# Table loads, weight narrowing and first folds moved in the opening steps of an FNet and gated-convolution kernel

## Chip, cores, metric

The kernel runs on one core of a Trainium2 chip. The metric is the device time of one execution in microseconds (us), given as the median of several executions. A profiled execution is read from its trace, whose times count from the start of the span. In the profile PE is TensorE (PEld its weight loads), DVE is VectorE, ACT is ScalarE and POOL is GpSimd. PSUM is where the program's matrix products are put.

## The reference

The reference takes the real part of a two-dimensional Fourier transform of `x` (8 batches, 3136 positions, 256 features), multiplies by `w_in` (256 x 1024), applies relu, a three-tap convolution over positions with a sigmoid, the gate, and `w_out` (1024 x 256):

```python
X = np.fft.fft(np.fft.fft(x, axis=1), axis=2).real
h = np.maximum(X @ w_in, 0.0)                  # 8 x 3136 x 1024
conv = sum(conv_w[k] * shifted(h, k - 1) for k in range(3))
out = (h / (1.0 + np.exp(-conv))) @ w_out      # 8 x 3136 x 256
```

The inputs of the weights are float64 in memory and are narrowed to float32 on the chip.

## The kernel before

A batch goes through folding on VectorE (sums and differences of mirrored positions), nine transform units on TensorE with tables of cosines and sines (four for odd, four for even frequencies, one for a single feature), and then 32 steps of the feed-forward part: 4 chunks of positions times 8 blocks of features. The 8 x 32 = 256 steps are one pipeline. In cycle t each engine does a piece of steps t - 3 to t + 2, and work of the next batch, and at first of the weights, is put in at given cycles:

```python
for t in range(n + LAG):                       # LAG is 3
    ...
    products(steps[t + 1]); copies(steps[t + 1])   # PE, then ACT
    combine(steps[t])                              # DVE: relu(h), frees a PSUM buffer
    ...
    run("dve")                                     # narrowing and folds
    ...
    other_taps(steps[t - 1]); gate(steps[t - 2])   # DVE, and GpSimd for half of gate
    mm2(steps[t - 3])                              # PE: times w_out
    run("pe")                                      # blocks(i), transform of the next batch
```

A weight is narrowed by seven integer and float instructions of VectorE. `w_in` is narrowed in four quarters. `blocks(i)` then multiplies quarter i with the small feature transform `dm`, so that the feed-forward part can start from the sequence transform. `w_out` is narrowed in four quarters too, and `mm2` of the first eight steps needs one of them every second step. The parts that the change touches, cut:

```python
for par in (1, 0):                 # odd tables, then even tables
    load_tables(par)
    if par:
        w_in[0].load(nc.sync)
        nc.sync.dma_start(out=dm, in_=dft_dim[:, :, 0:2])
for i in (1, 2, 3):
    w_in[i].load(nc.sync)
...
keep_on(18)                        # dummy matmuls, meant to keep PE's clock up
mirror_tables(0); mend_row(1, half); mirror_tables(2)     # ACT, odd tables: fill in, scale one row
for i in range(4):
    for j, u in enumerate(odds):
        u.part(i)
        if i == 3:
            u.copy(); u.fin()      # ACT; DVE, frees the unit's PSUM buffer
            if j == 1:
                ...
                w_in[0].narrow(0, 2)
mend_row(0, half)                  # ACT, even tables
for i, u in enumerate(us[j] for j in (2, 4, 3, 7, 8)):
    u.matmuls(0, 1); u.copy(); u.fin()
    if i == 2:
        ...
        blocks(0)
keep_on(2)
w_in[1].narrow(0, 2)
...
for i in (1, 2, 3):
    if i > 1:
        at(2 * i - 2, "dve", lambda i=i: w_in[i].narrow(0, 2))
    at(2 * i - 2, "pe", lambda i=i: blocks(i))
for c in range(0, NF, 2):
    at(1 + c, "dve", lambda c=c: w_out.narrow(c, c + 2))
...
end = 5                            # first cycle with a fold of the next batch
```

In what follows "step 6" or "combine(6)" counts such cycles, and "first product" is the first matmul of step 0.

## Time and profile before

| | before |
|---|---|
| median of 3 runs | 1252.91 us (1252.37 to 1253.13) |
| PE, DVE, ACT, GpSimd busy, share of the span | 97%, 91%, 71%, 32% |
| first product of step 0 | 44.20 us |
| combine(19), right behind the last fold of batch 1 (step 18) | 157.19 us |

The page has the span in 40 slices of 31 us. Each digit is the busy share of a slice in tenths, and for PEclk the granted clock of PE:

```profile
PE   5999999999999999999999999999999999999998
...
DVE  6799989999999999998999988999999888899996
...
PEclk9989999999999999999999999999999999999999
```

PE and DVE are both over 90% nearly everywhere, so neither alone can be called the bound from this view. The third digit of PEclk, from 62 to 94 us, is the one place where the clock was not at its full speed for long (0.50 from 62.5 to 69.3 us). That is in the stretch that the change touches. Which engine sets the time in which part of it is read from the timelines, which the prediction shows.

### The profile page before, as it was taken

The numbers are of one execution on the slowest core, as the hardware profiler recorded it, in microseconds if no ns is written. First come the engines' busy times: TensorE is split into PE (matmuls) and PEld (weight loads), VectorE is DVE, ScalarE is ACT, GpSimd is POOL, SyncE is SP. The second block draws the span as 40 slices with busy tenths as digits, with TensorE's granted clock in tenths as the row PEclk, the third lists the DMA queues.
The fourth block names the chain that finished last, engine by engine and source line by source line (L and its number), as shares of the span: only waits on it lengthen the run. The fifth ranks groups of instructions, "written<-read, shape, count | busy, mean of one in ns | idle before, by whom it ended". The sixth has DMA issues, their size and how long they took to land.

```text
span 1250.0 us, 15703 instructions
## 1 busy us (share of the span) xinstructions
PE 1206.5 (97%) x4982; PEld 906.1 (72%) x4982; DVE 1140.6 (91%) x1691; ACT 885.1 (71%) x1843; POOL 398.1 (32%) x502
## 2 busy tenths in 40 slices
PE   5999999999999999999999999999999999999998
PEld 4557776677777767777677777777777777777776
DVE  6799989999999999998999988999999888899996
ACT  2436666776777776777777777777777778788885
POOL 5214432442524151332424215242322213122222
PEclk9989999999999999999999999999999999999999
DMA  9503121220302021110202012020010001100000
GB/s 237 162 1 96 34 78 57 73 70 9 97 33 82 26 69 29 59 52 26 91 32 62 28 52 71 26 85 26 1 45 33 30 26 40 32 28 31 26 26 29
DMA packets 47618, 65.86 MB, mean 53 GB/s; under 512 B 5740, under 2 KB 35204, under 8 KB 47536
## 3 DMA queue, kind: packets, MB, share of 16 engines
q1 hardware_dynamic: 42355, 51.98, 13.5%
q0 software_dynamic: 5120, 12.85, 3.6%
q8 instruction: 39, 0.64, 0.2%
q14 instruction: 43, 0.35, 0.1%
q10 hardware_dynamic: 61, 0.04, 0.0%
HBM read 39.06 MB, written 25.74 MB: 52 GB/s over the span
## 4 chain that ended last, share of the span: by engine, by line
PE 65%; DVE 20%; issue 5%; ACT 5%; POOL 1%; DMA 1%; SPq 0%; DVEq 0%; ACTq 0%; POOLq 0%
PE po L91 40%; PE pb L91 10%; PE pa L91 9%; DVE g L604 7%; PE pd L91 6%; DVE g L625 3%; DVE h L592 3%; ACT nb L581 2%; DVE xh L166 1%; ACT g L617 1%; DVE xh L155 1%; DVE w L182 1%; DVE w L183 1%; DVE xh L170 1%; DVE xh L171 1%
## 5 line engine op out<-in xcount | busy, mean ns | idle before, releaser
L91 PE MATMUL po<-wout,g 128*128 128x256 f32 x3072 | 711.0, 381 | 20.2 <-DVE g L625 16.3
L91 PEld LDWEIGHTS po<-wout,g 128*128 128x128 f32 x3072 | 577.4, 190 | 178.3 <-DVE g L625 53.1
L604 DVE SCALAR_TENSOR_TENSOR g<-h,cw,g 128x770 f32<-128x770 f32 (+1 forms) x512 | 555.3, 1084 | 10.7 <-ACT g L598 1.5
L624 POOL TENSOR_TENSOR g<-g,h 128x385 f32<-128x385 f32 (+1 forms) x256 | 240.5, 940 | 747.6 <-ACT g L617 525.9
L617 ACT ACTIVATE g<-g 128x385 f32<-128x385 f32 (+2 forms) x512 | 244.3, 527 | 200.6 <-DVE g L604 200.4
L581 ACT ACTIVATE nb<-pb 128x386 f32<-128x386 f32 (+2 forms) x472 | 208.1, 494 | 82.6 <-PE pb L91 81.2
L592 DVE CUSTOM_DVE_ANT_0 h<-pa,nb 128x386 f32<-128x386 f32 (+2 forms) x492 | 255.4, 559 | 5.3 <-ACT h L578 5.3
L598 ACT ACTIVATE g<-h,cw 128x770 f32<-128x770 f32 (+1 forms) x256 | 243.4, 951 | 0.2 <-DVE h L592 0.2
L91 PE MATMUL pb<-qt,G 127*128 127x387 f32 (+2 forms) x512 | 214.1, 499 | 0.4 <-ACT nb L581 0.2
L91 PE MATMUL pa<-pt,G 128*128 128x387 f32 (+2 forms) x512 | 211.8, 494 | 0.0
L625 DVE TENSOR_TENSOR g<-g,h 128x385 f32<-128x385 f32 (+1 forms) x256 | 151.8, 593 | 1.3 <-ACT g L617 1.3
L91 PEld LDWEIGHTS pa<-pt,G 128*128 128x128 f32 x512 | 96.9, 189 | 73.5 <-issue 18.9
L547 ACT ACTIVATE pa<-eb,ge 128x387 f32<-128x387 f32 (+2 forms) x248 | 149.2, 602 | 0.6 <-PE pa L91 0.6
L91 PE MATMUL pd<-tab,w 98*128 98x196 f32 (+3 forms) x448 | 117.4, 374 | 0.0
L91 PEld LDWEIGHTS pb<-qt,G 127*128 127x128 f32 x512 | 93.9, 190 | 22.6 <-issue 4.0
L130 POOL DMA_INDIRECT xh<-in_x_dram,idx x64 | 97.8, 1528 | 15.4 <-issue 12.2
L91 PEld LDWEIGHTS pd<-tab,w 98*128 98x128 f32 (+1 forms) x448 | 82.9, 190 | 12.8
L644 ACT COPY os<-po 128x256 f32<-128x256 f32 x196 | 58.0, 396 | 10.6 <-PE po L91 5.8
L155 DVE TENSOR_TENSOR xh<-xh 98x1020 f32<-98x1020 f32 (+1 forms) x32 | 45.7, 1433 | 2.4 <-DMA xh<-in_x_dram,idx 2.4
L166 DVE TENSOR_TENSOR xh<-xh 98x1024 f32<-98x1024 f32 (+1 forms) x32 | 41.4, 1294 | 0.1
L285 DVE TENSOR_TENSOR qt<-as,pd 128x197 f32<-128x197 f32 (+1 forms) x14 | 7.3, 519 | 24.9 <-ACT as L281 24.9
L347 POOL TENSOR_TENSOR er<-as 1x197 f32<-1x197 f32 (+1 forms) x16 | 12.5, 778 | 52.5 <-ACT as L339 46.0
(100 smaller groups left out, 456.6 us busy)
## 6 DMA issues: line engine op xcount, KB each, us to landing
out_dram<-os SPq DMA_DIRECT2D x192, 128.0 KB
xh<-in_x_dram SPq DMA_DIRECT2D x16, 784.0 KB
eb<-ed SPq DMA_DIRECT2D x16, 193.5 KB
tab<-dft_seq_dram SPq DMA_DIRECT2D x4, 589.5 KB
raw<-in_moe_w_in_dram SPq DMA_DIRECT2D x4, 512.0 KB
raw<-in_moe_w_out_dram SPq DMA_DIRECT2D x1, 2048.0 KB
eb<-ed SPq DMA_DIRECT2D x8, 209.0 KB
eb<-ed SPq DMA_DIRECT2D x7, 193.0 KB
```

The source lines that it names most:

```text
L91: nc.tensor.matmul(o, l, r, start=start, stop=stop, skip_group_check=True)
L130: nc.gpsimd.indirect_dma_start(out=xh[b, h][0:NP, 7 - m].rearrange("p q d -> p (q d)"), out_offset=None, in_=bass.AP(tensor=x.tensor, offs ...
L155: vt(a[:, :, :, 1:D], a[:, :, :, 1:D], r[:, :, :, D - 1:0:-1], op=ALU.add)
L547: act(pa[s][:, 0:n], eb[b, c], AF.Copy, scale=ge[:, f:f + 1])
L581: act(nb[s][:, i, cols], p[:, cols], AF.Copy, scale=-1.0 if i else 1.0)
L592: nc.vector._custom_dve(TENSOR_ADD_SAT, out=to, in0=a[:, cols], in1=c[:, i, cols], s0=BIG, s1=0.0)
L598: act(gs[s], hs[s][:, 0:n], AF.Copy, scale=cw[:, 0, s[2]:s[2] + 1])
L604: stt(out=g, in0=h[:, k:k + n], scalar=cw[:, k, f:f + 1], in1=g, op0=ALU.mult, op1=ALU.add)
L617: act(gs[s][:, c], gs[s][:, c], AF.Sigmoid)
L624: gt(g[:, p], g[:, p], h[:, p], op=ALU.mult)
L625: vt(g[:, v], g[:, v], h[:, v], op=ALU.mult)
L644: nc.scalar.copy(out=osb[:, j % 2], in_=pt[:, j % 2])
```

## The change

The intent is to remove idle time of PE and DVE in the first 160 us. The even tables are loaded directly behind the odd ones, so that `mend_row(0)` can run on ScalarE ahead of the odd units. `w_in`'s first quarter is narrowed behind all odd units, and `blocks(0)` runs behind all units. The third and fourth quarters, until now narrowed in the step of their blocks, are narrowed two and three steps ahead of them, `w_out`'s quarters one step later, and the folds of batch 1 begin at step 7 instead of 5.

```diff
     for par in (1, 0):
         load_tables(par)
-        if par:
-            w_in[0].load(nc.sync)
+    for i in range(4):
+        w_in[i].load(nc.sync)
+        if i == 0:
             nc.sync.dma_start(out=dm, in_=dft_dim[:, :, 0:2])
-    for i in (1, 2, 3):
-        w_in[i].load(nc.sync)
...
-    keep_on(18)
+    keep_on(16)
     mirror_tables(0)
     mend_row(1, half)
     mirror_tables(2)
+    mend_row(0, half)
...
                     w_out.load(nc.sync)
-                    w_in[0].narrow(0, 2)
-    mend_row(0, half)
+    w_in[0].narrow(0, 2)
     for i, u in enumerate(us[j] for j in (2, 4, 3, 7, 8)):
...
             for f in load_ops(1, 0, nc.sync):
                 f()
-            blocks(0)
-
-    keep_on(2)
+    blocks(0)
     w_in[1].narrow(0, 2)
...
         if i > 1:
-            at(2 * i - 2, "dve", lambda i=i: w_in[i].narrow(0, 2))
+            at(i - 2, "dve", lambda i=i: w_in[i].narrow(0, 2))
         at(2 * i - 2, "pe", lambda i=i: blocks(i))
     for c in range(0, NF, 2):
-        at(1 + c, "dve", lambda c=c: w_out.narrow(c, c + 2))
+        at(2 + c, "dve", lambda c=c: w_out.narrow(c, c + 2))
...
-    end = 5
+    end = 7
```

## The prediction

> **What bounds the kernel now.** The change touches only the start: the loads of the tables and of w_in, the first two transforms, and the first nineteen of 256 steps. So I first asked the page for its chain of work that ended last, then the same chain in order of time, then the timelines of TensorE (PE), VectorE (DVE) and ScalarE (ACT) up to 160 us, one engine at a time, and granted clocks in 2 us windows.
>
> Over the whole span PE carries the chain:
>
> ```profile
> PE 65%; DVE 20%; issue 5%; ACT 5%; POOL 1%; DMA 1%; SPq 0%; DVEq 0%; ACTq 0%; POOLq 0%
> ```
>
> In order of time it passes through PE, ACT and DVE by turns until 95.7 us, is DVE without a gap from 96.3 to 157 us, and then mostly PE. All that follows 157 us is placed relative to the steps and the change doesn't move it, so what is won by there should reach the end unchanged. The question is when DVE gets to step 19, and I look for idle time ahead of that on PE and DVE.
>
> TensorE's timeline before (start us, length, instructions, idle just before and its releaser):
>
> ```profile
> 13.46 10.31 PE L91 MATMUL pb<-w 98*128 98x256 f32 x36 [6.74 <-POOL w L184]
> 23.60 8.10 PE L91 MATMUL po<-tab,w 98*128 98x196 f32 x32
> 32.67 1.67 PE L91 MATMUL po<-tab,w 99*128 99x197 f32 x8 [0.96 <-ACT tab L227]
> ...
> 50.25 2.85 PE L91 MATMUL po<-win,dm 128*128 128x256 f32 x12
> ...
> 63.74 5.58 PE L91 MATMUL po<-win,dm 128*128 128x256 f32 x12 [2.69 <-DVE win L427]
> ```
>
> The first line is keep_on: 18 dummies [...], 10.31 / 18 = 0.57 us each. The odd products come right behind them at 23.60. ScalarE shows that the odd tables had landed before that (it waits for that load and starts at 22.75), so the dummies delay PE by about 0.8 us. At 32.67 PE waits 0.96 us for mend_row(0). At 63.74 it waits 2.69 us until DVE has narrowed w_in's third quarter, and then blocks(2) takes 5.58 us where blocks(1), with the same 12 matmuls, took 2.85. The windows (busy us of PE, PEld, DVE, ACT, POOL, then PEclk) say why, the clock is halved:
>
> ```profile
> 62.00:64.00 2.00, 0.26 (x1) 0.26 (x2) 1.97 (x3) 1.31 (x3) 0.41 (x1) 0.61 0.02 4
> 64.00:66.00 2.00, 2.00 (x5) 1.59 (x6) 1.97 (x3) 0.14 (x1) 0.00 (x0) 0.50 0.03 8
> ```
>
> VectorE before, its idle places and the two marks I count with (combine of steps 6 and 19):
>
> ```profile
> 42.18 0.51 DVE L285 TENSOR_TENSOR pt<-as,po 128x197 f32<-128x197 f32 x1 [2.39 <-ACT as L281]
> ...
> 51.03 0.56 DVE L592 CUSTOM_DVE_ANT_0 h<-pa,nb 128x385 f32<-128x385 f32 x1 [2.13 <-ACT h L578]
> ...
> 90.73 0.56 DVE L592 CUSTOM_DVE_ANT_0 h<-pa,nb 128x385 f32<-128x385 f32 x1 [0.74 <-ACT h L578]
> ...
> 157.19 0.55 DVE L592 CUSTOM_DVE_ANT_0 h<-pa,nb 128x386 f32<-128x386 f32 x1
> ```
>
> The 2.39 us are there because blocks(0) stands on PE ahead of the last two units of the transform. From 90.73 on DVE idles only 0.68 us more; so step 19 comes at 157.19 because of DVE's work behind combine(6).
>
> [...] Here each step has one DVE instruction some 0.55 us too long when GpSimd's gate runs (1.24 instead of 0.69 us for one of the narrowing steps at 61.72). The change keeps one such meeting a step, so I count nothing for it.
>
> **The change, part by part.**
>
> *Loads.* The even tables (2 x 589.5 + 24.6 + 12.3 KB = 1.22 MB) pass ahead of w_in's first quarter and dm (0.77 MB). The windows from 20 to 32 us show about 265 GB/s, so the even tables land about 0.77 / 265 = 2.9 us earlier. By estimate that is 22.75 + 1.22 / 265 = 27.4 us, and w_in 0 and dm near 30.3. First uses: mend_row(0) on ACT, when mirroring ends at 27.8; narrowing w_in 0, below at 33.0. Both in time, narrowly for the first. No time by itself; it permits the next.
>
> *keep_on(16) and no keep_on(2).* Two dummies fewer are 1.15 us, so PE is free at 22.5 and the odd products start when the tables are there, at about 22.85: 0.75 us won. The other two (1.02 us at 43.0) filled an idle wait.
>
> *Order of the first transform.* mend_row(0) now runs in ACT's idle time before the odd copies: its 0.96 us of PE wait goes. blocks(0) and the narrowing of w_in 0 move behind the odd units, blocks(0) behind all units. PE back to back: 22.85 + 8.10 odd products + 6.97 even and feature units (1.59 + 0.81 + 1.66 + 2.91, start to start) + 2.75 blocks(0) = 40.7 for the first product of step 0, against 44.20. DVE: fins of the odd units from 29.7 to 33.0, narrowing 3.95 us, four even fins at 0.70 to 39.8; ACT's flip, behind GpSimd's feature rows, may add 0.5. So both are free about 3.5 us earlier for PE, 4 for DVE.
>
> *Narrowing two steps ahead.* Narrowing is seven instructions: 0.42 + 0.43 + 0.43 + 0.69 + 0.43 + 0.69 + 0.69, with gaps 3.95 us. w_in 2 now comes in step 0, by 49.1, and blocks(2) is reached at 40.7 + 16.7 = 57.4: the wait of 2.69 goes, and with it the slow clock, 6.43 us to the next product against 3.67 for the same work warm: 2.76.
>
> *PE up to the first product of step 6:* 3.5 + 2.69 + 2.76 = 8.95 us earlier, at 77.9 instead of 86.88. blocks(3) keeps its three waits (1.4 us) for the one free PSUM buffer.
>
> *DVE up to combine(6).* At combine(5), 74.0, after it taps and a gate to 77.6; combine(6) can't come before PE's product and ACT's copy, 90.73 - 8.95 = 81.8. DVE idles 4 us there. So up to step 6 PE sets the time.
>
> *DVE from combine(6) to combine(19).* Before: 157.19 - 90.73 = 66.46, less 0.68 idle = 65.8 of work. The same steps now hold also what was moved behind: one quarter of w_out (two quarters, steps 6 and 8, instead of the one of step 7), 3.95, and the first fold (steps 7 instead of 5; the second fold was behind combine(6) anyway), 1.13. 65.8 + 5.1 = 70.9, with no idle. 81.8 + 70.9 = 152.7, 4.5 us before 157.19. PE, freed at step 9 some 9 us earlier, needs about 4.55 us a step against DVE's 4.7 and more, so it waits for DVE and doesn't set this.
>
> The sum: 8.95 won by PE, 5.1 given back by work moved into DVE's full stretch, 0.7 of idle removed: 4.5 us, or 0.36%. 1252.9 - 4.5 = 1248.4. I add 0.3 for small waits that I can't see (GpSimd's memset of h behind four row gathers that now run beside narrowing): **1248.7 us**.
>
> **Rivals.**
> 1. *DVE bounds the stretch from 44 to 157 altogether.* For: its chain has no gap from 96 us. Then the wait and cold clock of PE at 61 to 70 were hidden and only the earlier start counts, 3.5 less 1 to 3 for folds moved out of room into the full stretch: 1250 to 1252. Against: DVE itself waits for PE at 74.02, 90.73 and 96.31 (0.56, 0.74, 0.68).
> 2. *A load takes the place of the removed wait.* If the even tables land after 27.8, mend_row(0) holds ACT's in-order queue, and with it the copies of the odd units; each us late is a us lost on DVE and PE. Landing at 30 would make it about 1250.5. If w_in 0 came after 33.0, likewise.
> 3. *The later folds cost nothing and DVE has more room than counted* (the 4 us of idle at step 6 get filled): up to 3 us more, 1246.
> 4. *Another slow clock.* PE now has some 8 us of waits spread over steps 9 to 19. No single one nears 2.7 us, so I give it little; if it happened, 3 to 5 us lost.
>
> **Range and chances.** The total at stake, all idle time of DVE between 30 and 157 us, is 8.6 us (3.3 in the transform, 5.3 after), 0.7% of the time, so 2% (25 us) is out of reach either way unless something breaks. Runs of before lie within 0.8 us. Rivals 1 and 2 set the high end, 1251.2; rival 3 the low end, 1246.4. Faster by over 2%: 0.01; within 2%: 0.98; slower: 0.01.
>
> **What would show it.** The odd products start near 22.85; ACT shows no DMA wait for mend_row(0); the first pb product is near 40.7; no idle before blocks(2) and clock 1.00 from 56 to 72; DVE idles about 4 us before combine(6), near 81.8, and never more than fractions until combine(19), near 152.7; from there the two timelines differ by a constant. It is wrong if combine(19) is not 3 to 6 us earlier, or if the difference there doesn't reach the end, which a load or transform placed by time rather than by step would cause.

## The result, and the profile after

The median of 4 runs after is 1248.95 us (1248.73 to 1249.92), beside 1252.8 us before (now 4 runs): 3.85 us or 0.3% less. The ratio is 0.9971 with a 95% interval of 0.9954 to 0.9988. A second set of 6 runs, on the chip of the last experiments, gave 1249.26 us beside 1252.12 us, ratio 0.9976 (0.9960 to 0.9992). So the gain is about 3 to 4 us (2.86 and 3.85). By the 2% measure the kernels are the same.

PE's timeline of the changed kernel (start us, length, instructions, idle just before and its releaser), the places that the prediction named:

```profile
13.33 10.07 PE L91 MATMUL pb<-w 98*128 98x256 f32 x32 [6.86 <-POOL w L178]
23.24 9.51 PE L91 MATMUL po<-tab,w 98*128 98x196 f32 x40
...
33.49 4.47 PE L91 MATMUL po<-tab,w 99*128 99x196 f32 x24
39.16 2.92 PE L91 MATMUL po<-win,dm 128*128 128x256 f32 x12 [1.19 <-ACT as L281]
42.00 0.92 PE L91 MATMUL pb<-qt,G 127*128 127x386 f32 x2
...
58.72 2.85 PE L91 MATMUL po<-win,dm 128*128 128x256 f32 x12
```

The first line ends at 23.4: the 16 dummies took nearly as long as the 18 before. The wait for `mend_row(0)` is gone: odd and even units now run on in one line. A new wait of 1.19 us stands before `blocks(0)`, so the first product is at 42.00, not at 40.7. The wait before `blocks(2)` is gone, and with it the slow clock: these are the same windows as those of before (PE, PEld, DVE, ACT, POOL busy, then PEclk, DMA share and GB/s).

```profile
62.00:64.00 2.00, 2.00 (x10) 1.18 (x11) 1.97 (x4) 0.16 (x1) 0.00 (x0) 1.00 0.03 8
64.00:66.00 2.00, 2.00 (x7) 1.13 (x8) 2.00 (x3) 1.58 (x4) 0.97 (x2) 1.00 0.00 0
```

ScalarE's timeline after has the one wait for a load that the new order brought:

```profile
28.68 1.13 ACT L227 ACTIVATE tab<-tab,half 2x393 f32<-2x393 f32 x2 [1.06 <-DMA tab<-dft_seq_dram]
29.83 0.32 ACT L300 COPY as<-po 128x196 f32<-128x196 f32 x1
```

The even tables landed at about 28.7, 1.3 us later than estimated, and the first copy of an odd unit stands directly behind `mend_row(0)`.

VectorE's timeline after: the last three of the seven instructions that narrow `w_in`'s first quarter, then the idle places and the two marks:

```profile
35.68 0.65 DVE L425 TENSOR_SCALAR raw<-raw 128x512 int32<-128x512 int32 x1
36.37 0.90 DVE L426 SCALAR_TENSOR_TENSOR raw<-raw 128x512 f32<-128x512 uint32 x1
37.30 0.98 DVE L427 SCALAR_TENSOR_TENSOR win<-raw,win 128x512 f32<-128x512 f32 x1
...
42.11 0.60 DVE L420 TENSOR_SCALAR win<-raw 128x512 int32<-128x512 int32 x1 [0.90 <-issue]
...
80.33 0.92 DVE L624 TENSOR_TENSOR g<-g,h 128x385 f32<-128x385 f32 x1 [2.55 <-ACT g L616]
82.97 0.56 DVE L591 CUSTOM_DVE_ANT_0 h<-pa,nb 128x385 f32<-128x385 f32 x1 [1.73 <-ACT h L577]
...
154.14 0.56 DVE L591 CUSTOM_DVE_ANT_0 h<-pa,nb 128x386 f32<-128x386 f32 x1
```

Those three took 0.43, 0.70 and 0.69 us before. At 42.11 DVE had stood 0.90 us: the next quarter lies in the same buffer as the one that `blocks(0)` is still reading (the profile names no releaser here; for the same wait in b_both it names PE's `po`, which `blocks(0)` writes). Before combine(6), at 82.97, it was idle for 2.55 + 1.73 = 4.28 us. Between combine(6) and combine(19) it had no wait.

From step 20 on the traces differ by a constant. The first product of step 20 comes 3.06 us earlier than before, that of step 64 3.01, of step 128 3.15, and of step 250 3.08; the spans differ by 1250.0 - 1246.9 = 3.1. So the gain is made before step 19 and kept.

### The profile page after: what moved, and what is told of

The parts are those of the page before. It is cut to its first block, busy times and chain, and to the rows that moved or that the text cites. A ratio compares the mean times of both kernels' runs of the same rounds, so it can differ in the third digit from the quotient of the medians.

```text
span 1246.9 us, 15694 instructions
## 1 busy us (share of the span) xinstructions
PE 1202.5 (96%) x4974; PEld 903.8 (72%) x4974; DVE 1140.9 (92%) x1691; ACT 885.6 (71%) x1843; POOL 396.0 (32%) x502
## 4 chain that ended last, share of the span: by engine, by line
PE 65%; DVE 21%; issue 5%; ACT 4%; POOL 2%; DMA 2%; SPq 0%; DVEq 0%; POOLq 0%; ACTq 0%
PE po L91 40%; PE pb L91 10%; PE pa L91 9%; DVE g L603 7%; PE pd L91 7%; DVE g L624 3%; DVE h L591 3%; ACT nb L580 2%; DVE xh L166 1%; DVE xh L155 1%; POOL xh L130 1%; DVE w L182 1%; ACT g L616 1%; DMA tab<-dft_seq_dram 1%; DVE w L183 1%
## 5 line engine op out<-in xcount | busy, mean ns | idle before, releaser
L130 POOL DMA_INDIRECT xh<-in_x_dram,idx x64 | 96.5, 1508 | 19.4 <-issue 12.8
```

The lines of the kernel that those rows point to most:

```text
L130: nc.gpsimd.indirect_dma_start(out=xh[b, h][0:NP, 7 - m].rearrange("p q d -> p (q d)"), out_offset=None, in_=bass.AP(tensor=x.tensor, offs ...
```

## Experiments

Twelve kernels were run, each with 6 executions beside the kernel before, and each gave the right result. Differences below 2 us are within the intervals of the ratios, so for these the verdict rests on marks in the traces (us from the span's start):

| run | first product | product of step 6 | combine(6) | combine(19) | first product to combine(19) | median us |
|---|---|---|---|---|---|---|
| before | 44.20 | 86.88 | 90.73 | 157.19 | 112.99 | 1252.91 |
| after | 42.00 | 79.12 | 82.97 | 154.14 | 112.14 | 1248.95 |
| a_front | 42.46 | 84.18 | 88.03 | 154.54 | 112.08 | 1250.33 |
| a_narrow | 44.79 | 81.87 | 85.73 | 155.03 | 110.24 | 1250.42 |
| a_fold7 | 45.50 | 87.15 | 91.01 | 160.27 | 114.77 | 1255.26 |
| b_fold5 | 42.54 | 79.66 | 83.51 | 152.80 | 110.26 | 1247.83 |
| b_wout | 42.56 | 79.67 | 83.53 | 152.79 | 110.23 | 1247.67 |
| b_both | 42.48 | 79.60 | 86.05 | 153.25 | 110.77 | 1245.68 |
| b_loads | 47.08 | 84.20 | 88.05 | 159.23 | 112.15 | 1254.12 |
| c_early | 43.72 | 82.51 | 89.16 | 153.43 | 109.71 | 1249.72 |
| after_again | 42.62 | 79.74 | 83.59 | 154.76 | 112.14 | 1249.26 |
| d_psum | 41.76 | 78.88 | 82.73 | 153.90 | 112.14 | 1248.69 |
| d_blocks3 | 43.47 | 78.89 | 86.49 | 151.96 | 108.49 | 1245.92 |
| d_best | 41.81 | 77.23 | 84.80 | 150.26 | 108.45 | 1245.15 |

The first product itself varies between executions. The odd tables land at different times (22.57 us in the trace after, 23.91 in that of d_blocks3), and the dummies ahead of the odd units end at different times: before, a_narrow and a_fold7 have the same front part, and their odd units begin at 23.60, 24.19 and 24.89 us though the tables were there at 22.75, 22.73 and 23.22. So the column of distances is the more telling one.

The theory was that PE sets the time up to combine(6) and VectorE from there to combine(19). The rival was that VectorE bounds the whole stretch, so that only its own earlier start counts.

### a_front: the front part alone

```diff
 (the changed kernel with)
-            at(i - 2, "dve", lambda i=i: w_in[i].narrow(0, 2))
+            at(2 * i - 2, "dve", lambda i=i: w_in[i].narrow(0, 2))
-        at(2 + c, "dve", lambda c=c: w_out.narrow(c, c + 2))
+        at(1 + c, "dve", lambda c=c: w_out.narrow(c, c + 2))
-    end = 7
+    end = 5
```

> The kernel before with only the front part of the change: table loads first, mend_row(0) before the odd units, both narrowing of w_in 0 and blocks(0) moved, 16 and no late dummies. Narrowing and folds as before. Theory (PE sets the time up to combine of step 6, VectorE from there to step 19): the first product comes at 42.0 us instead of 44.2, the wait before blocks(2) and its slow clock stay, so everything shifts by 2.2 us: 1250.6. Rival (VectorE bounds all of 44 to 157 us): the first narrowing behind the transform also comes 2.2 us earlier, and this alone carries the whole gain of the change, 1249.0.

Measured: 1250.33 us, beside 1252.49 before, ratio 0.9974 (0.9959 to 0.9989). That is 2.2 us less. PE still stood before `blocks(2)`:

```profile
62.03 4.59 PE L91 MATMUL po<-win,dm 128*128 128x256 f32 x12 [2.70 <-DVE win L427]
```

The wait is the old one, 2.70 us, and the clock fell again (0.52 from 64 to 66 us). The slow clock cost less this time, 4.59 instead of 5.58 us: by the clock records of the traces it lasted 3.41 us here and 6.83 us in the trace before. One of the six executions, 1247.71 us with a mean clock of 0.999 over the span instead of 0.997 to 0.999 in the others, was 2.4 us shorter than the next. The front part is worth about 2.2 us in the median and not the whole gain. This run does not tell the theory from the rival by itself: with the shorter slow clock its distance to combine(19), 112.08 us, is no longer than that of the changed kernel, 112.14, and its trace loses another 1.3 us between the products of steps 64 and 70, which d_best will show again. The next two runs decide between them.

### a_narrow: the narrowing alone

```diff
 (the kernel before with)
-            at(2 * i - 2, "dve", lambda i=i: w_in[i].narrow(0, 2))
+            at(i - 2, "dve", lambda i=i: w_in[i].narrow(0, 2))
-        at(1 + c, "dve", lambda c=c: w_out.narrow(c, c + 2))
+        at(2 + c, "dve", lambda c=c: w_out.narrow(c, c + 2))
```

> The kernel before with only the narrowing of w_in 2 and 3 moved to steps 0 and 1 and w_out's quarters to steps 2, 4, 6, 8. Theory: PE loses its 2.69 us wait and the 2.76 us of slow clock, so combine(6) comes 5.45 us earlier (85.3), one more quarter of w_out (3.95) then stands behind it and 0.7 of idle goes: 2.2 us faster, 1250.6, with granted clock 1.00 from 56 to 72 us and about 4 us of VectorE idle before combine(6). Rival (VectorE bounds the stretch): its work is the same and only changes order, so no gain, 1252.8.

Measured: 1250.42 us, ratio 0.9979 (0.9966 to 0.9993), 2.1 us less. All six executions had a clock of 1.000, the distance from the first product to that of step 6 fell from 42.68 to 37.08 us, and DVE idled 1.48 + 1.73 us before combine(6), somewhat less than the 4 expected. VectorE's work was the same and in another order, so the rival, which expected no gain, fell.

### a_fold7: the later folds alone

```diff
 (the kernel before with)
-    end = 5
+    end = 7
```

> The kernel before with only the folds begun at step 7 instead of 5. Theory: the first two fold instructions (1.13 and 1.13 plus 0.84 us) leave places where VectorE waits for PE anyway and are added behind combine(7): 1.5 to 3 us slower, 1254.3 to 1255.8. Rival (VectorE bounds the stretch): the same work before step 19, no difference, 1252.8.

Measured: 1255.26 us, ratio 1.0022 (1.0006 to 1.0037), 2.8 us more. In the trace the distance from the first product to combine(19) grew by 1.8 us. This is what the folds cost; the first product of this execution was also 1.30 us later, ahead of anything that the edit touches, so part of the 2.8 is chance. The waits of DVE before combine(6) and combine(7) grew from 0.74 and 0.68 to 1.21 and 1.72 us. The folds had filled time in which DVE waited for PE; at step 7 they do not.

### b_fold5: the changed kernel with the old start of the folds

```diff
 (the changed kernel with)
-    end = 7
+    end = 5
```

> The changed kernel with the folds begun at step 5 again. Theory: the first fold instruction fits into VectorE's 4.3 us of idle before combine(6), which now runs from 77.8 to 82.97 us, so combine(19) and the end come 1.1 to 1.3 us earlier: 1247.8. Rival (the later folds are part of the gain, since they keep VectorE free while PE catches up): 1 to 3 us slower than the changed kernel.

Measured: 1247.83 us, ratio 0.9964 (0.9948 to 0.9980), so 1.1 to 1.4 us below the two medians of the changed kernel. In the trace the distance to combine(19) is 1.9 us shorter (110.26 against 112.14), and DVE's idle before combine(6) fell from 4.28 to 1.41 + 1.74 = 3.15 us. This part of the change takes back some of what the others win. Two of the six executions had a clock of 0.995 and took 1249.7 and 1250.84 us; the other four lie between 1247.02 and 1248.29.

### b_wout: the third quarter of w_out in the idle time (and the fourth a step earlier)

```diff
 (the changed kernel with)
-    for c in range(0, NF, 2):
-        at(2 + c, "dve", lambda c=c: w_out.narrow(c, c + 2))
+    for c, t0 in zip(range(0, NF, 2), (2, 4, 5, 7)):
+        at(t0, "dve", lambda c=c: w_out.narrow(c, c + 2))
```

> The changed kernel with w_out's quarters narrowed in steps 2, 4, 5, 7 instead of 2, 4, 6, 8; folds from step 7 as in the change. Theory: the third quarter (3.95 us) goes into VectorE's idle of 4.3 us before combine(6), so it no longer stands behind it: combine(6) stays at about 40.97 us after the first product and combine(19) comes about 3.9 us earlier, 1245.0. Rival (the idle is a limit by something else, or VectorE's later work hides behind PE): no gain, 1249.

Measured: 1247.67 us, ratio 0.9956 (0.9943 to 0.9970). The expectation for combine(6) held to the hundredth, 83.53 - 42.56 = 40.97 us behind the first product, but the gain is about half of what was expected. VectorE's timeline shows what took its place:

```profile
83.53 0.56 DVE L591 CUSTOM_DVE_ANT_0 h<-pa,nb 128x385 f32<-128x385 f32 x1 [0.30 <-ACT h L577]
84.35 2.56 DVE L603 SCALAR_TENSOR_TENSOR g<-h,cw,g 128x770 f32<-128x770 f32 x2 [0.27 <-ACT g L597]
89.11 0.56 DVE L591 CUSTOM_DVE_ANT_0 h<-pa,nb 128x385 f32<-128x385 f32 x1 [1.72 <-ACT h L577]
```

Where DVE has no quarter to narrow in step 6, it is ready for combine(7) before PE is: 0.30 + 0.27 + 1.72 = 2.29 us of idle. PE sets the time up to step 7 here. The border between the two bounds moves with the work.

### b_both: the two together

```diff
 (b_wout with)
-    end = 7
+    end = 5
```

> The same and folds from step 5. Theory: the idle before combine(6) is used up by the quarter alone, so of the 1.9 us that the earlier folds gave on top of the change only some 0.5 remain: 1244.5. Rival (folds and quarter are independent gains): 1249 - 3.9 - 1.9 = 1243.2.

Measured: 1245.68 us, ratio 0.9938 (0.9925 to 0.9952). This beats both kernels, by 7 us against before. It lies 1.2 us above the theory's 1244.5 and further from the rival's figure. The profiled execution, at 1247.93 us the longest of the six, is worth a look, for the windows show a clock that was halved without a long wait (PE, PEld, DVE, ACT, POOL busy, then PEclk):

```profile
74.00:76.00 2.00, 1.54 (x8) 1.03 (x7) 1.97 (x4) 0.37 (x1) 0.10 (x1) 1.00 0.00 0
76.00:78.00 2.00, 1.54 (x8) 0.57 (x6) 1.90 (x5) 0.37 (x1) 0.00 (x0) 1.00 0.00 0
78.00:80.00 2.00, 1.55 (x11) 1.19 (x10) 1.90 (x4) 0.59 (x3) 0.00 (x0) 0.97 0.00 0
80.00:82.00 2.00, 2.00 (x4) 0.67 (x2) 2.00 (x3) 1.26 (x3) 1.56 (x1) 0.50 0.00 0
```

These are the three waits of 0.46 us in `blocks(3)`. They were followed by 6.83 us at half clock (79.88 to 86.70), and the step from product 6 to product 7 took 8.95 us (79.60 to 88.55) instead of 5.66. The other five executions, with clocks of 0.999 or 1.000, took 1244.72 to 1245.99 us.

### b_loads: the old order of loads

```diff
 (the changed kernel with)
     for par in (1, 0):
         load_tables(par)
-    for i in range(4):
-        w_in[i].load(nc.sync)
-        if i == 0:
+        if par:
+            w_in[0].load(nc.sync)
             nc.sync.dma_start(out=dm, in_=dft_dim[:, :, 0:2])
+    for i in (1, 2, 3):
+        w_in[i].load(nc.sync)
```

> The changed kernel with the old order of loads (w_in's first quarter and dm ahead of the even tables) and mend_row(0) still ahead of the odd units. Theory: 0.77 MB more in front at about 265 GB/s bring the even tables 2.9 us later (31.6 instead of 28.7), ScalarE stands before mend_row(0) until then, the first copy and with it VectorE's chain come 2.9 us later, 1251.9: the new order of loads is what permits the early mend_row. Rival (the order of loads is immaterial, since the copies have slack): 1249.

Measured: 1254.12 us, ratio 1.0010 (0.9996 to 1.0024), 5 us above the changed kernel, so worse than either the theory or the rival had it. `mend_row(0)` began at 32.30 us, 3.6 us later than in the changed kernel, and PE stood for 3.26 us before the even units:

```profile
34.53 2.15 PE L91 MATMUL po<-tab,w 99*128 99x197 f32 x8 [3.26 <-DVE as L306]
36.62 1.48 PE L91 MATMUL pd<-tab,ea 99*1 99x197 f32 x16
38.03 6.44 PE L91 MATMUL po<-tab,w 99*128 99x196 f32 x24
```

The clock was 0.50 from 35.5 to 42.3 us: the last line took 6.44 us, and 4.47 in the changed kernel. The later load and the slow clock that its wait brought make 5.08 us at the first product, and this arrives whole at combine(19), 159.23 against 154.14. So the order of loads is what permits the early `mend_row(0)`. Of the miss of 2.2 us in size (5.1 against 2.9), 0.7 is the load itself, 3.6 us late and not 2.9, and the rest came with the slow clock.

### c_early: an attempt to beat b_both

```diff
 (b_both with the old order of loads, and)
     mirror_tables(2)
-    mend_row(0, half)
+    w_in[0].narrow(0, 2)
...
-    w_in[0].narrow(0, 2)
+    mend_row(0, half)
+    blocks(0)
     for i, u in enumerate(us[j] for j in (2, 4, 3, 7, 8)):
         u.matmuls(0, 1); u.copy(); u.fin()
+        if i == 0:
+            w_in[1].narrow(0, 2)
...
-    blocks(0)
-    w_in[1].narrow(0, 2)
...
+        if b == 1:
+            cs = [3, 4, 5, 7, 8, 9, 10, 12, 13, 14, 15, 16, 17, 18]
```

> An attempt to beat both. From the previous-but-one with: old order of loads, the first quarter of w_in narrowed in VectorE's idle time before the odd units (26 to 30 us), mend_row(0) behind the odd units and blocks(0) on PE in the meantime, the second quarter narrowed behind the first even unit, and the first folds at steps 3, 4, 5. Theory: 3.2 us of VectorE work moves into idle time at the start, PE's first product stays near 42.5, and the fold instructions fill what room this makes before combine(6): about 1241.5. Rival (PE sets it from here, or the even tables at 31.6 hold the even units): 1244 to 1246.

Measured: 1249.72 us, ratio 0.9978 (0.9961 to 0.9994). It failed. The narrowing placed between two even units held the fin that PE's first product needs:

```profile
43.72 1.56 PE L91 MATMUL pb<-qt,G 127*128 127x386 f32 x2 [1.52 <-DVE qt L285]
```

PE waited 1.52 us, its clock was 0.50 from 43.8 to 47.2 us, the first step took 4.77 us (43.72 to 48.49) instead of 3.09, and DVE then idled 3.94 us before combine(0). The dummies that the kernel before had just there, `keep_on(2)`, were missing; whether they would have held the clock was not tried.

### after_again and d_psum: why the first product was late

> The changed kernel once more, unaltered, to have it on the same chip as the next three and with more runs: 1249.0, most of its runs with a granted clock of 0.999 or 1.000; a run whose clock is 0.996 or less should be 2 to 4 us longer.

Measured: 1249.26 us, all six clocks 0.999 or 1.000. So no execution tests the second half of the sentence.

In d_psum `blocks(0)` gets its PSUM buffers from the pools of the steps, not from the four that the units use:

```diff
 (the changed kernel with)
+    def own(j):
+        if j < 2:
+            return psa.tile([P, 512], F32, name="pa", tag="pa")
+        return psd.tile([P, 512], F32, name="pd", tag="pd")
...
-            p = spare()
+            p = spare() if i else own(g)
...
-        p = spare()
+        p = spare() if i else own(2)
```

> The changed kernel with blocks(0) writing into the PSUM buffers of the steps (which are free then) instead of those of the transform. It tests why the first product came at 42.0 and not at the predicted 40.7. Theory: PE stands 1.2 us before blocks(0) because the first even unit's fin, which frees the PSUM buffer, queues on VectorE behind narrowing w_in 0 (38.2 to 39.05). With another buffer PE starts when the narrowing ends, 0.9 us earlier, and so does VectorE's next narrowing, which waits for blocks(0): first product 0.9 us earlier, 1248.1. Rival (what the profile names holds it: ScalarE's last copy, which waits for GpSimd's feature rows): first product unchanged, 1249.

Measured: 1248.69 us, ratio 0.9974 (0.9959 to 0.9990), with one execution of 1251.08 us at a clock of 0.996. The first product came at 41.76 us, 0.86 earlier than in after_again on the same chip, and the marks behind it up to combine(19) are 0.86 earlier too, though the narrowing began within 0.1 us of the same time (34.13 and 34.20 us). In the medians, 0.6 us apart, the two do not differ beyond the noise. PE now starts right behind the narrowing:

```profile
38.88 1.99 PE L91 MATMUL pa<-win,dm 128*128 128x256 f32 x8 [0.56 <-DVE win L427]
```

So the wait of 1.19 us in the changed kernel was for the PSUM buffer, which the first even unit's fin freed on VectorE behind the narrowing (its last instruction ran from 38.55 to about 39.05). The releaser that the profile named there, a copy of ScalarE that ended 0.05 us later, was only the last to end before the start: in d_psum PE starts 0.46 us before that copy does (39.34 us). The next narrowing's wait of 0.90 us for `blocks(0)` went as well.

### d_blocks3 and d_best: without waits for one PSUM buffer

```diff
 (b_both with)
-        at(2 * i - 2, "pe", lambda i=i: blocks(i))
+        at(2 * (i > 1), "pe", lambda i=i: blocks(i))
-    for c, t0 in zip(range(0, NF, 2), (2, 4, 5, 7)):
+    for c, t0 in zip(range(0, NF, 2), (2, 3, 5, 7)):
...
+        if b == 1:
+            cs = [4, 5, 6, 7, 8, 9, 10, 12, 13, 14, 15, 16, 17, 18]
 (d_best: and with d_psum's edit)
```

> The version with folds from 5 and w_out in 2, 4, 5, 7, which in some runs lost 2 to 3 us to a halved clock right behind blocks(3). Now blocks(3) stands behind blocks(2) in step 2, where all four PSUM buffers are free, w_out is narrowed in 2, 3, 5, 7 and the first fold is in step 4. Theory: PE's three waits of 0.46 us before step 6 go and with them the slow clock there, VectorE has no wait from step 3 to 19: 1245.0 with every run's clock at 0.998 or above and a spread under 1 us. Rival (the slow clock comes from elsewhere): as before, 1244.7 to 1247.9.

> The two together. VectorE has no wait behind the transform, so the 0.9 us of the earlier start should arrive whole: 1244.1. Rival (PE sets the time again somewhere before step 9): 1245.

Measured: d_blocks3 1245.92 us (1245.08 to 1246.75), ratio 0.9948 (0.9933 to 0.9964); d_best 1245.15 us (1244.68 to 1246.37), ratio 0.9943 (0.9928 to 0.9959). Both have no wait of PE from the first product to step 9 and none of DVE from step 0 to 19, and all twelve executions have clocks of 0.999 or 1.000. The spread is 1.7 us, below b_both's 3.2 but not below 1. Their medians do not differ from b_both's beyond the noise, so no gain in the median is shown. That the halved clock behind `blocks(3)` is removed is not shown either: of the kernels with `blocks(3)` in step 4 and no wait before `blocks(2)` or the even units (the changed kernel twice, b_fold5, b_wout, b_both, d_psum), 4 of 34 executions had a clock of 0.996 or less, and of these two 0 of 12, which at that share would come about by chance one time in five.

d_best reaches combine(19) 1.70 us earlier than d_blocks3, of which 1.66 us stand in its earlier first product. Its median is nearer to the rival's 1245 than to the 1244.1 of the theory, but not for the rival's reason. Its profiled execution, at 1246.37 us its longest, lost 1.3 us again between the products of steps 64 and 70, where PE waited 1.45 us for a ScalarE copy at 389 us; in the trace before the same wait is 0.21 us. That copy was late because ScalarE, ahead of it, had waited before the seventh of seven copies of outputs (the lines of before, a_front and d_best, in this order):

```profile
392.62 0.37 ACT L644 COPY os<-po 128x256 f32<-128x256 f32 x1 [2.15 <-DMA out_dram<-os]
391.30 0.37 ACT L643 COPY os<-po 128x256 f32<-128x256 f32 x1 [3.41 <-DMA out_dram<-os]
387.02 0.37 ACT L648 COPY os<-po 128x256 f32<-128x256 f32 x1 [3.37 <-PE po L91]
```

For twelve of the fourteen traces this wait is 1.93 to 2.15 us, and the releaser is the store of an earlier output, which frees the buffer that the copy writes. In a_front and d_best it is about 1.3 us longer, and PE then waits 1.49 and 1.45 us. In d_best the profile names PE instead, but the product that this copy reads ended at 383.04 us there, so the store is the likelier cause. Why the store landed later in these two executions is left open.

## Why the prediction was right

*Total.* 1248.7 us was predicted, 1248.95 and 1249.26 were measured. The mechanism held, with one term mis-sized by 1.3 us. That the total came so close is in part luck: in the traces combine(19) came 3.05 us earlier and not 4.5, at the edge of the "3 to 6 us" that the prediction set itself as a condition (2.43 in after_again's trace, which is from another set of runs than the trace before). The added 0.3 us and the difference between profiled and timed executions made up for part of that. Two of its smaller signs failed: the odd products began at 23.24 us and not near 22.85, and ScalarE did wait for a DMA before `mend_row(0)`.

*PE sets the time up to step 6, VectorE from there to 19.* Right. DVE idled 4.28 us before combine(6), where 4 was predicted, and not at all from there to combine(19). a_narrow gave 2.1 us by order alone, and a_fold7 lost 1.8 us of its trace by order alone; the rival in these experiments (VectorE bounds the stretch) expected nothing from either. The third rival, that the later folds cost nothing, fell with a_fold7 and b_fold5, which show 1.8 and 1.9 us.

*Wait of 2.69 and slow clock of 2.76 us at blocks(2).* Right. Both went. Product 6 came 7.76 us earlier, 2.20 of it from the first product, so 5.56 from there on, where 5.45 was worked out. The slow clock lasted 6.83 us in the trace before; what it cost is the 2.76.

*70.9 us of work from combine(6) to combine(19).* Right: 154.14 - 82.97 = 71.17. The 5.1 us moved into this stretch were given back as predicted, and b_fold5 and b_wout each show about 1.9 us of it taken out again.

*"So both are free about 3.5 us earlier for PE": this is the term that was mis-sized.* The first product came 2.20 us earlier, and DVE's next narrowing 2.25 instead of 4 (42.11 against 44.36). PE did reach the end of its even units at 33.49 + 4.47 = 37.96, as the sum had it (37.9). What failed was "PE back to back" from there to `blocks(0)`: the sum had the narrowing finished and a PSUM buffer free by then. Three things were left out. The odd copies and fins began 0.5 us later (30.18 on DVE instead of 29.7): 0.4 of it because the dummies ended later than expected, 0.1 because the even tables landed 1.3 us late. The narrowing took 4.6 instead of 3.95 us, with GpSimd's feature rows beside it. And the buffer that `blocks(0)` takes is freed by a fin queued behind that narrowing. d_psum took the last of these away and got 0.86 us; the other two were not tried one by one.

*"0.57 us each" for the dummies.* Wrong: 16 took 10.07 us where 18 took 10.31. The figure is an average over two speeds. In the trace before, their matmuls (two for each dummy) start 0.43 us apart until 17.9 us and 0.22 from 18.2; after, 0.43 until 19.0 and 0.22 from 19.4. The trace's first clock record, full speed, begins at 18.09 and at 19.24 us, so by estimate the slower pace is the half clock that the trace before shows later, where twelve matmuls of `blocks(2)` took 5.58 us and not 2.85; the window column reads 1.00 there for want of a record. Two dummies fewer are then 0.86 us at the faster pace and not 1.15, and as the faster pace came 1.15 us later in this execution they freed PE only 0.36 us earlier.

*"One meeting a step, so I count nothing" for GpSimd.* Right for the steps, wrong for the transform, where the narrowing was moved beside the feature rows (0.72 us more on three instructions).

*The second rival, a late load.* It was there in small: ScalarE waited 1.06 us for the even tables, and the copy behind `mend_row(0)` followed without a gap, but by estimate this cost only 0.1 us: before, that copy waited for PE until 30.09 us with odd units begun at 23.60; begun at 23.24, PE would have let it start at 29.73, and it started at 29.83. b_loads shows that 3.6 us more would have cost 5 us: there the first copy stood behind `mend_row(0)` until 33.45 us.

*The fourth rival, another slow clock.* Not in the ten executions of the changed kernel, but in single executions of its relatives. In b_both it followed three short waits, which the prediction had called unlikely because no single one was long; the same three waits brought none in the trace after (clock 1.00 from 74 to 82 us).

*The difference reaches the end.* Right: 3.06 us at step 20, 3.08 at step 250.

## What to carry to other kernels

Where two engines are both over 90% busy, find which of them waits for the other in each stretch, and place movable work in front of the point at which the roles change: here a quarter of a weight and a fold, 5.1 us by the prediction's sum, gave back more than half of the 7.8 us that PE had won, and moving them into the 4.3 us of idle time before step 6 was worth more than 3 us again. Moving work ahead on an engine can also delay what frees a buffer behind it (here 0.86 us at the first product, by d_psum); ask for each moved piece which buffer's last reader now queues behind it. A wait of PE is dearer than its length where a halved clock follows it: here 2.69 us of wait and 2.76 us of slow work.

## What the runs show of clock, GpSimd and loads

- A halved clock (0.50) followed a single wait of PE of 2.69 us (before, where the clock fell 1.4 us after PE's last matmul), 2.70 us (a_front, a_fold7), 3.26 us (b_loads) and 1.52 us (c_early), and, in one execution of b_both, three of 0.46 us within 5 us with matmuls between them. But 1.19 us (after) and 1.38 us (d_blocks3) before `blocks(0)` were not followed by one, nor were the same three of 0.46 us in the trace after, so the runs give no length that is safe. The half clock lasted 3.4 us in the traces of a_front and c_early and 6.8 us in those of before, b_both and b_loads. The first record of the full clock begins 4.6 us (before) and 5.9 us (after) behind the start of the first dummy.
- With GpSimd instructions on a single partition (1 x 196 and 1 x 197 elements) beside them, three instructions of narrowing on 128 partitions took 0.65, 0.90 and 0.98 us instead of 0.43, 0.70 and 0.69.
- With 0.77 MB moved behind the even tables, these could be used 3.6 us earlier (28.68 us in the changed kernel, 32.30 us in b_loads). The estimate of when they land, 27.4 us, took loads to land in the order of issue at the mean rate, about 265 GB/s; it was 1.3 us too early.
